# One more batch turned by DMA in a planned attention and mixture-of-experts kernel, with truer turn times in its planner and a new step order

## Chip, cores, metric

One core of one Trainium2 chip. The metric is the device time of one execution in microseconds (us). Where several runs are quoted, it is their median. All outputs are right.

The engines: PE is TensorE, PEld its weight loads, DVE VectorE, ACT ScalarE, POOL GpSimd, SPq the DMA queue of SyncE. A turn is a transposition by DMA, issued from SyncE. Small turns make xT (the attention output, turned) and rT (K and Q of the last 64 tokens), large ones make qkT (K and Q of half a batch).

## The reference, cut to what matters

```python
def phi(x):                                   # q, k, v: 8 batches, 8 heads, 576 tokens, 64 columns
    proj = x @ w_phi                          # 64 -> 128
    proj = proj - max(abs(proj), axis=-1)
    return concat([exp(proj), exp(-proj)])
num = q_p @ (k_p.T @ v);  den = q_p @ sum(k_p)
x = (num / den).transpose(0, 2, 1, 3).reshape(4608, 512)
P = exp(x @ w_gate)                           # 8 rounds of row and column normalisation follow
out = sum over 8 experts e of  P[:, e] * (relu(x @ w1[e]) @ w2[e])
```

Attention has to be finished before the routing is known. Expert 0's matmuls need no routing, though, so the kernel mixes them into the attention as filling for TensorE (PE).

## The kernel before

Each step of the algorithm (one letter of a string) appends operations to a plan. A list scheduler in the kernel then fixes at build time the order in which each engine gets its instructions. So the order is frozen on the chip: an engine stands at the next instruction of its list until that one can go.

```python
class Links:                                   # the planner's model of the DMA queues
    ...
            a, b = (x[0][2] for x in self.line)
            all_ = (0.61 if a.turn else 0.84) / (a.unit + b.unit)
    ...
    def dma(queue, nbytes, rate, fn, r=(), w=()):
        speed, unit = LINK.get(rate, (rate, 40))
        ...
        o = plan.op(queue, 0.8 if queue == "POOL" else 0.6, 0.0, fn, r, w, (), nbytes / speed)
        o.turn, o.unit = rate == 148, unit
    ...
    def pair_c(b, pr, xb):                     # turns a head pair's attention output into xT
        if b in (3, 4, 5, 6,):
            dma("SP", 1 << 17, 148, lambda: nc.sync.dma_start_transpose(
                out=xT[:, pr, b * SM:(b + 1) * SM].rearrange("p (a c) -> p a c", c=128),
                in_=xb()[:, 0:NJ].rearrange("p a b -> p (a b)")), [(xb, 0), (xb, 1)], [("xT", b, pr)])
            return
        pxt = new("P1")
        for j in range(NJ):                    # four transposes on PE
            pe(128, lambda j=j: nc.tensor.transpose(
                bf(pxt)[:, j * 128:j * 128 + 128], xb()[:, j, :], ident), ...)
        dve(270, lambda: nc.vector.tensor_copy(out=xT[:, pr, ...], in_=bf(pxt)[:, 0:512]), ...)
    ...
    def load_qk(b, hh, nh, t, r=()):           # K and Q of half a batch; from batch 2 on POOL's queue
        ...
            dma("POOL", nh << 17, 230, lambda x=x, src=src: nc.gpsimd.dma_start(
                out=t["qk"]()[:, x, o:o + nh], in_=...), r, [(t["qk"], x, i) for i in keys])
    def turn_qk(t, pr=None):                   # turns them into qkT on SyncE, one large DMA
        ...
            dma("SP", 1 << 19, 148, lambda: nc.sync.dma_start_transpose(
                out=t["T"]()..., in_=t["qk"]()...), ...)
    ...
    def gates():                               # a load is held until these have run
        seen = order[:at[0]]
        return [("max", x, seen.count(n) - 1) for x, n in ((0, "q"), (1, "a")) if n in seen]
    def stage_l(n):
        b, i = 1 + n // 2, n % 2
        if b > 1:
            halves[b, i] = new_half(b, i)
        load_qk(b, 4 * i, 4, halves[b, i], gates())
        load_v(b, 4 * i, 4, halves[b, i], gates())
    ...
    order = (
        "lraeaepqbwlqaqawwabwmqlltnrbppnwqbppmrmanbqaqmwwacmpnpbccpwbtcnmqnaqbclupunm"
        ...
```

The K and Q loads stand in POOL's list between POOL's own arithmetic (a negation `m`, a multiply `v`), which ACT and PE need. And their target `qk` is a ring buffer: a load may go out only when the turn that reads the buffer's earlier content has landed.

The softmax here doesn't subtract the row's maximum and nothing guards it: scores larger than these inputs give would overflow.

## Time and profile before

| | before |
|---|---|
| time | 1027.87 us, 3 runs from 1026.58 to 1027.88 |
| span of the profiled run | 1026.8 us |
| busy share PE / DVE / ACT / POOL | 98 / 80 / 69 / 45 % |
| turns by DMA, of attention outputs | 16 of 1.19 us on SyncE |

Busy shares average over two regimes: up to some 210 us attention feeds PE through DVE, ACT and POOL; after 262 us PE is full and nothing else counts. What a change in the first regime is worth can only be read there, from what PE waits for. The lines are in the prediction below.

### The profile page before, as it was taken

Reading aid. Unit: us, or ns where it says so; the run is one execution under the profiler, and the core shown is the slowest. Engines: PE = TensorE matmul, PEld = TensorE weight load, DVE = VectorE, ACT = ScalarE, POOL = GpSimd, SP = SyncE. Lnnn points to the kernel's source line nnn. Section 1 sums busy time; section 2 is a strip of 40 time slices with the busy share of each in tenths; the row PEclk is TensorE's granted clock in tenths of the full one; section 3 lists DMA queues with packets and bytes.
Section 4 is the critical chain, followed back from the end, with each engine's and each line's share of the span. In section 5 each row is a group of like instructions: output and inputs, shape, how many; then the busy total and the mean of one; then the engine's idle time right before and its main releaser. Section 6 shows DMA issues by size and latency. Waiting matters only on the chain.

```text
span 1026.8 us, 24281 instructions
## 1 busy us (share of the span) xinstructions
PE 1008.1 (98%) x9469; PEld 837.9 (82%) x9504; DVE 823.5 (80%) x1600; ACT 703.9 (69%) x1530; POOL 458.5 (45%) x480
## 2 busy tenths in 40 slices
PE   7899999999999999999999999999999999999998
PEld 4666666645888888888888888888888888888886
DVE  7999989987888887787777877787778877787775
ACT  7999999834888766666666666666665666666663
POOL 5768664400334444444444434544444433444342
PEclk9999999999999999999999999999999999999999
DMA  9999978170232611161115211341116111614333
GB/s 235 192 197 179 177 137 130 37 154 19 85 104 85 124 42 42 47 129 43 48 46 112 54 43 42 75 102 42 42 46 131 42 42 43 130 36 125 133 124 124
DMA packets 112501, 96.03 MB, mean 94 GB/s; under 512 B 54145, under 2 KB 87041, under 8 KB 112385
## 3 DMA queue, kind: packets, MB, share of 16 engines
q1 hardware_dynamic: 80576, 70.55, 26.5%
q0 software_dynamic: 31648, 23.86, 16.6%
q8 instruction: 74, 1.21, 0.5%
q14 instruction: 43, 0.34, 0.1%
q10 hardware_dynamic: 160, 0.07, 0.0%
HBM read 94.98 MB, written 14.16 MB: 106 GB/s over the span
## 4 chain that ended last, share of the span: by engine, by line
PE 93%; ACT 2%; DVE 1%; DMA 1%; SPq 1%; issue 1%; POOL 0%; DVEq 0%; ACTq 0%
PE ps L1273 74%; PE ps L573 17%; PE ps L856 2%; DMA acc<-in_q_dram 1%; ACT q L569 1%; ACT k L569 0%; SPq L495 0%; ACT wx L569 0%; SPq L551 0%; PE ps L885 0%; DMA xd<-S 0%; DVE ps L864 0%; DVE hT L1305 0%; DVE m L565 0%; POOL wx L761 0%
## 5 line engine op out<-in xcount | busy, mean ns | idle before, releaser
L1428 POOL TENSOR_TENSOR acc<-acc,V 128x512 f32<-128x512 f32 x248 | 314.8, 1280 | 484.5 <-ACT V L1425 426.7
L1301 ACT COPY U<-ps 128x512 f32<-128x512 f32 x378 | 217.0, 586 | 166.2 <-PE ps L1273 150.9
L1305 DVE CUSTOM_DVE_ANT_0 hT<-ps,U 128x512 bf16<-128x512 f32 x378 | 254.6, 687 | 87.7 <-PE ps L1273 59.9
L1425 ACT ACTIVATE V<-ps,P 128x256 f32<-128x256 f32 x496 | 208.1, 473 | 90.7 <-PE ps L1273 82.1
L1413 DVE SCALAR_TENSOR_TENSOR acc<-ps,P,acc 128x256 f32<-128x256 f32 x372 | 159.1, 478 | 69.5 <-PE ps L1273 69.2
L1273 PEld LDWEIGHTS <-S 128*128 128x128 bf16 x1984 | 194.1, 98 | 22.6 <-issue 0.2
L1273 PEld LDWEIGHTS <-T 128*128 128x128 bf16 x1512 | 148.0, 98 | 17.2
L1273 PEld LDWEIGHTS <-hT 128*128 128x128 bf16 x1488 | 145.6, 98 | 16.8
L1273 PE MATMUL ps<-X,T 128*128 128x256 bf16 x1008 | 152.4, 273 | 0.0
L1273 PE MATMUL ps<-T,S 128*128 128x256 bf16 x1056 | 135.8, 273 | 0.0
L1273 PEld LDWEIGHTS <-wx 128*128 128x128 bf16 x1152 | 112.7, 98 | 13.6 <-issue 0.2
L1181 DVE TENSOR_TENSOR S<-hT 128x1024 bf16<-128x1024 bf16 x124 | 87.2, 712 | 10.1 <-ACT hT L1310 9.9
L1273 PEld LDWEIGHTS <-w 128*128 128x128 bf16 x864 | 84.5, 98 | 9.8
L1273 PE MATMUL ps<-xT,wx 128*128 128x256 bf16 x576 | 88.4, 273 | 0.1
L1273 PE MATMUL ps<-X,wx 128*128 128x256 bf16 x576 | 86.8, 273 | 0.0
L1310 ACT ACTIVATE hT<-ps 128x512 bf16<-128x512 f32 x126 | 73.2, 606 | 9.8 <-PE ps L1273 9.8
L1273 PE MATMUL ps<-wx,hT 128*128 128x256 bf16 x560 | 77.6, 273 | 0.0
L1273 PE MATMUL ps<-xT,T 128*128 128x256 bf16 x504 | 76.7, 273 | 0.0
L573 PE MATMUL ps<-xT,w 128*128 128x512 bf16 x270 | 70.5, 379 | 0.7
L573 PE MATMUL ps<-w,hT 128*128 128x512 bf16 x276 | 69.8, 379 | 0.7 <-ACT q L569 0.2
L1273 PE MATMUL ps<-T,hT 128*128 128x256 bf16 x496 | 69.2, 273 | 0.0
L1273 PE MATMUL ps<-xT,w 128*128 128x256 bf16 x432 | 66.5, 273 | 0.0
(129 smaller groups left out, 1426.5 us busy)
## 6 DMA issues: line engine op xcount, KB each, us to landing
X<-xd SPq DMA_DIRECT2D x126, 256.0 KB, 2.7
wx<-in_moe_w_dram POOLq DMA_DIRECT2D x8, 1024.0 KB, 12.4
v_m<-in_v_dram SPq DMA_DIRECT2D x15, 512.0 KB, 5.6
out_dram<-acc SPq DMA_DIRECT2D x14, 512.0 KB, 2.9
w<-in_moe_w_dram POOLq DMA_DIRECT2D x6, 1024.0 KB, 12.1
xd<-S SPq DMA_DIRECT2D x18, 256.0 KB, 2.1
qk<-in_k_dram POOLq DMA_DIRECT2D x12, 256.0 KB, 5.5
qk<-in_q_dram POOLq DMA_DIRECT2D x12, 256.0 KB, 6.4
```

Source lines behind the costliest of these rows:

```text
L569: act(el, lambda: nc.scalar.activation(out=dst(), in_=src(), func=ACT.Exp, bias=0.0, scale=scale), r, w)
L573: nc.tensor.matmul(out_, lhsT=lhsT, rhs=rhs, start=start, stop=stop)
L856: pe(65, lambda j=j: nc.tensor.matmul(pn()[:, j * D1:j * D1 + D1], lhsT=s["T"][x]()[:, j % 2, 2 * h + j // 2, :] if j < 4 else r["T"][x]() ...
L1181: lambda: f.tensor_tensor(out=out_(), in0=x(), in1=y(), op=op), r, w, **kw)
L1273: pe(256, lambda i=i, k=k, z=z: nc.tensor.matmul(bank()[:, 256 * i:256 * i + 256], lhsT=lhs(k, i), rhs=rhs(k), start=first and z, stop=k = ...
L1301: act(512, lambda: nc.scalar.copy(out=u[fp][n]().rearrange("p a b -> p (a b)"), in_=x[fp]()), [x[fp]], [u[fp][n]])
L1305: dve(515, lambda: nc.vector._custom_dve(ADD_SAT, out=out_(fp, i, j), in0=bank[fp]().rearrange("p (a b) -> p a b", a=2), in1=u[fp][n](), s ...
L1310: act(512, lambda: nc.scalar.activation(out=out_(fp, i, j), in_=x[fp]().rearrange("p (a b) -> p a b", a=2), func=ACT.Relu, bias=0.0, scale ...
L1413: dve(320, lambda n=n, ts=ts: nc.vector.scalar_tensor_tensor(out=acc[g][:, ts, 256 * j:256 * j + 256], in0=bank()[:, 256 * n:256 * n + 256 ...
L1425: act(370, lambda n=n: nc.scalar.activation(out=u()[:, n, :], in_=bank()[:, 256 * n:256 * n + 256], func=ACT.Copy, bias=0.0, scale=P[:, 4 ...
L1428: pool(695, lambda: nc.gpsimd.tensor_tensor(out=acc[g][:, 2 * i:2 * i + 2, 256 * j:256 * j + 256], in0=acc[g][:, 2 * i:2 * i + 2, 256 * j: ...
```

## The change

The intent was to take 16 transposes from PE, to let the planner know how long a turn really holds SyncE, and to search a step order for that plan.

```diff
-            all_ = (0.61 if a.turn else 0.84) / (a.unit + b.unit)
+            all_ = (0.56 if a.turn else 0.84) / (a.unit + b.unit)
...
-        o = plan.op(queue, 0.8 if queue == "POOL" else 0.6, 0.0, fn, r, w, (), nbytes / speed)
+        dur = 0.8 if queue == "POOL" else 0.6 if rate != 148 else 2.4 if nbytes > 1 << 18 else 1.25
+        o = plan.op(queue, dur, 0.0, fn, r, w, (), nbytes / speed)
...
-        if b in (3, 4, 5, 6,):
+        if b in (2, 3, 4, 5, 6,):
...
-        load_qk(b, 4 * i, 4, halves[b, i], gates())
-        load_v(b, 4 * i, 4, halves[b, i], gates())
+        held = gates() if n else []
+        load_qk(b, 4 * i, 4, halves[b, i], held)
+        load_v(b, 4 * i, 4, halves[b, i], held)
...
     order = (
-        "lraeaepqbwlqaqawwabwmqlltnrbppnwqbppmrmanbqaqmwwacmpnpbccpwbtcnmqnaqbclupunm"
+        "arpqbwaaelwqwleaanmqwcbpwpqlnwbbrpeaqmqammnnqbbbcarctwcpplmtpmunlqnwcpnbtuau"
...   (four more lines of the string, all different)
```

More of the change, by code (lines that the diff above doesn't have):

```diff
@@ L1053 @@
     order = (
-        "lraeaepqbwlqaqawwabwmqlltnrbppnwqbppmrmanbqaqmwwacmpnpbccpwbtcnmqnaqbclupunm"
-        "taumquglcapalbcpnqqdcenmucugbblnapmrcqdutabnqpmunpbambccddnqplanmqmducpblttb"
-        "augnaqlnrbdcampcadmqeutunqcppmdcaqtdqabpbbmlrqtdnpmuaqualbnagnacctbmqulupran"
-        "tdpmtdqcmdnpdabdancpcabbqmpumqbcdgnappqunburqcbugmmnqdcdanumupqbnucmcpnmbddp"
-        "bqmpncncubncmmgccg"
+        "arpqbwaaelwqwleaanmqwcbpwpqlnwbbrpeaqmqammnnqbbbcarctwcpplmtpmunlqnwcpnbtuau"
+        "aqcpqunldamqblapnmcctadtuapqlalbmbgrgnuapalqaubmbmtcuqmpnbcdmnpdaqbccdrtqupq"
+        "nubnlnuqempgccupmanaclpadtbmadcqbdmpnqtdrbtqbdcnpuqbmlpmnuglndqpnbcamdapqnbu"
+        "cauamdcmrtuqmdndqpbumacbpunmgdpacqnuqpdtpbmndacbcbcagqcnpnurqumubpqmmbnbamcd"
+        "dcupmqcgncpbncnmcg"
     )
```

## The prediction

> **What bounds the kernel now.** I read the page's first two parts first, for who is busy and when.
>
> ```profile
> PE 1008.1 (98%) x9469; PEld 837.9 (82%) x9504; DVE 823.5 (80%) x1600; ACT 703.9 (69%) x1530; POOL 458.5 (45%) x480
> PE   7899999999999999999999999999999999999998
> DVE  7999989987888887787777877787778877787775
> ACT  7999999834888766666666666666665666666663
> POOL 5768664400334444444444434544444433444342
> PEclk9999999999999999999999999999999999999999
> ```
>
> TensorE is at work in 98% of the span at the full clock. Only its first two slices (51 us) are below 9 tenths. The second view is the table of stretches, where I cut the front finely:
>
> ```profile
> 0.00:10.00 10.00, 6.08 (x32) 4.45 (x33) 6.29 (x12) 5.28 (x11) 1.30 (x8) 1.00 0.74 205
> 10.00:20.00 10.00, 7.08 (x46) 4.17 (x44) 8.57 (x15) 8.89 (x26) 9.37 (x14) 1.00 1.20 285
> 20.00:30.00 10.00, 8.35 (x121) 6.08 (x120) 9.16 (x21) 9.47 (x25) 5.66 (x13) 1.00 1.25 246
> 30.00:40.00 10.00, 7.92 (x102) 6.32 (x99) 9.63 (x22) 9.74 (x25) 7.41 (x12) 1.00 1.23 134
> 40.00:50.00 10.00, 9.06 (x110) 5.96 (x109) 9.88 (x24) 10.00 (x27) 7.84 (x15) 1.00 1.35 189
> 50.00:60.00 10.00, 9.47 (x122) 6.90 (x124) 9.96 (x26) 10.00 (x25) 8.35 (x14) 1.00 1.08 209
> 60.00:70.00 10.00, 9.57 (x130) 6.67 (x129) 9.49 (x22) 8.94 (x22) 7.02 (x11) 1.00 1.07 171
> 262.00:1027.00 765.00, 760.22 (x6931) 677.93 (x6929) 591.75 (x1063) 486.75 (x1018) 324.63 (x260) 1.00 0.30 76
> ```
>
> Columns: stretch, length, then busy us and instructions of PE, PEld, DVE, ACT and POOL, then clock, DMA share and GB/s. From 20 to 70 us DVE and ACT have hardly a free moment (DVE 48.1 and ACT 48.2 of 50 us) while PE has holes: there PE waits for the attention chain and has no expert matmul to put between. From 262 us on PE is full, and that is three quarters of the span.
>
> Busy time includes the modelled tail of each matmul, so I also took the distance from one matmul's start to the next in the trace's records. The medians are 56 ns for 128 bf16 columns, 109 ns for 256 and 216 ns for 512. With 25 ns for the smallest, 109 ns for the fp32 transposes and columns/2.4 + 2.5 ns for the rest, the matmuls sum to 989.3 us. The first starts at 3.7 us. The last starts 4.9 us before the end. What is over, 1026.8 - 989.3 - 3.7 - 4.9 = 28.9 us, is holes between starts: 10.8 us before 30 us, 20.3 us before 70 us, 28.4 us before 260 us, and 0.4 us in all the rest. Between 70 and 260 us it is a steady 0.2 to 0.9 us in each 10 us.
>
> The third view is who PE waited for, cut at 70 us. Up to there:
>
> ```profile
> PE ps L703 <- DMA acc<-in_k_dram: 3.7, 1, 3.7
> PE ps L573 <- DVE wx L565: 1.9, 3, 1.4
> PE ps L703 <- ACT em_r L569: 1.1, 1, 1.1
> ```
>
> The first is the first input (the lead of 3.7 us), the others are DVE and ACT. For 70 to 262 us the same view is empty: no wait of PE there is long enough to be listed. So a DMA turn, a late V load or a late weight load costs PE nothing visible after 70 us.
>
> **What the Trainium skill says.** "TensorE: Matmul & The Clock Gate", section Back-to-back issue gap, gives N/2.4 + 2.5 ns for an isolated stream and 81 ns at N=128 for weight-load/matmul pairs. The trace agrees with the first (56, 109, 216 ns), and not with the 81 ns: the transposes here have a weight load each and still stand 56 ns apart. "VectorE: DVE Perf Modes", section The three transpose paths, puts a 128x128 bf16 transpose at 390 ns on TensorE and 1309 ns by DMA; the trace has 219 ns as the latency on TensorE, and a DMA turn of four such blocks occupies SyncE for 1.19 us and lands after 4.2 us. "DMA: Bandwidth & Descriptors", section DMA Transpose (X-bar), says that the plain transpose is issued from Sync or Scalar only and that two transposing streams must not be in flight together; here all are on SyncE, before and after, so there is one stream. The same page, section Issuing engines are not separate DMA queues, calls the issue time usually small against the transfer; here it is not:
>
> ```profile
> L879 SPq DMA_TRANSPOSE xT<-xb x10: 1190/1194/1403, 96.0 to 189.9; - x10
> L518 SPq DMA_TRANSPOSE qkT<-qk x12: 1322/1867/4506, 45.4 to 171.8; - x12
> L637 SPq DMA_TRANSPOSE rT<-qk_r x6: 1189/1506/3892, 27.1 to 131.9; - x6
> ```
>
> These are shortest, median and longest ns on SyncE. The kernel's planner booked 600 ns for each, so its planned order was wrong by 0.6 us for a small turn and by 1.3 us for a median large one.
>
> **The change part by part.** (1) Batch 2's attention output is turned by DMA as batches 3 to 6 are. Counting the built programs: 16 transposes and their 16 weight loads leave PE, four 128x512 copies leave DVE, four DMA turns are added on SyncE; nothing else changes in number on any engine.
>
> ```profile
> L885 PE MATMUL ps<-ident,xb x40: 216/219/222, 39.3 to 195.7; 128*128 128x128 bf16 x40
> L888 DVE COPY xT<-ps x16: 383/415/426, 41.9 to 204.2; 128x512 bf16<-128x512 bf16 x16
> ```
>
> PE: 16 x 56 ns = 0.9 us of stream, in a stretch where PE is full: this reaches the end. DVE: 4 x 0.415 = 1.7 us, at 80 to 95 us where DVE is 95% busy but PE does not wait for it: little of it reaches the end. SyncE: 4 x 1.19 = 4.8 us more, spread over a queue that has gaps of 1 to 4 us between its turns: off the path.
>
> (2) The planner's turn times (1.25 and 2.4 us, and a lower joint rate while a turn is in flight) add no instruction. They move SyncE's order: turns and V loads are sequenced as they really run. No PE wait after 70 us names a DMA, so the direct worth is near zero.
>
> (3) The hold. In the kernel before, the K/V load of batch 1 stands first in the step order, so its hold list is empty anyway. In the changed one it stands tenth; without the new rule it would wait for a maximum. With the rule SyncE's first 24 issues are the same in both programs. So this part allows the new order and gains nothing by itself.
>
> (4) The new step order is what can move the front. I laid the durations of the trace before over both instruction orders (sums, no replay). In front of the first expert up-projection stand 26.0 us of PE stream before, 25.3 after; of ACT records 57.7 and 56.5 us; and in front of the last batch 0 copy that it needs, 44.6 and 45.3 us of DVE records. In front of the eighth group: PE 38.6 and 37.9, ACT 75.0 and 71.9. In front of the twelfth: PE 50.3 and 52.9, ACT 90.3 and 93.5. Batch 1's last copy has 70.8 us of DVE records ahead before, 65.0 after. So the first group starts about when it did (46.3 us now), the middle comes some 2 to 3 us earlier on ACT, and the twelfth is even. The order reshuffles the front more than it shortens it. Also, the first weight load of expert 0 now goes out on POOL's queue ahead of the rest loads of batches 2 and 3, so the weights can't be the thing that is late; that queue's traffic at 10 to 20 us is not larger.
>
> Sum: 0.9 us of PE stream, plus 0 to 2 us fewer holes before 70 us (I choose 0.7, since the DVE count gets 0.7 longer while the ACT count gets up to 3 shorter), plus 0.2 us in the stretch from 70 to 205 us. 1027.9 - 1.8 = 1026.1 us.
>
> **The rivals.** (a) The front is shortened in earnest: if the holes before 70 us fall from 20.3 to about 17 us, as the ACT count at the eighth group allows at most, the sum is 0.9 + 3.3 = 4.2 us and the time 1023.7. For it: that order was searched with truer times. Against it: the DVE count in front of the first group, and that DVE and ACT are full there in any order. (b) A new wait takes the gain: a turn lands 4.2 us after issue and queues behind large turns that hold SyncE for up to 4.5 us, so xT of batch 2 comes some 4 to 8 us after its attention is done instead of about 1 us (0.22 + 0.42, with the waits). If PE then has nothing else, it shows as a wait on a DMA at 80 to 110 us; I allow 1 to 2 us, and the time would be 1027 to 1028. Against it: the list of PE's waits is empty there now, with 16 turns in the same queue. (c) The weight load that goes out earlier competes with the batch 1 loads, when the DMA share is already above 1 (two queues at once). Should the first transposes of the second half of batch 0 come 1 to 2 us later, everything shifts by that: 1027 to 1028. (d) Nothing moves after 205 us: routing on DVE and the first split products follow with PE full; a shift of 1 us either way leaves PE full.
>
> **Range and chances.** 0.9 us is sure. Around it lie the front (-3.3 to +2) and the queue (0 to +2). That gives 1023.3 to 1028.6 for 8 times in 10. 2% is 20.6 us, as large as all holes before 70 us together; PE's stream of 988.4 us can't shrink. So faster by 2% has a chance of 0.005, slower by 2% (a stall of 20 us) 0.01, within 2% 0.985.
>
> **What would show it right or wrong.** PE count down by 16, DVE by 4, 20 xT turns of 1.19 us on SyncE. The stretches 0 to 70 us: PE idle within 1.5 us of now (12.5 us), DVE and ACT still full. PE's waits after 70 us: still none of note; a wait on xT or rT from a DMA there would prove (b). First expert matmul at 45 to 48 us; if it comes before 44 us, (a); if after 49 us, (c). From 262 us on: the same 765 us. The prediction is wrong if the front's holes change by more than 3 us.

## The result, and the profile after

Before 1027.2 us (6 runs, 1026.36 to 1027.88), after 1028.82 us (6 runs, 1028.09 to 1031.25). A ratio here and below is the mean time of one kernel's fast runs over that of the other's fast runs of the same rounds, so it is not quite the ratio of the medians. It is 1.002, 95% interval 1.0007 to 1.0033. By the 2% measure that is "same", as predicted, but the sign is wrong and 1028.82 lies 0.2 us outside the range. The change costs about 2 us instead of saving 1.8.

Busy parts and slices of the changed kernel (this profiled run was the slowest of its six):

```profile
PE 1009.2 (98%) x9449; PEld 837.6 (81%) x9488; DVE 824.0 (80%) x1596; ACT 704.5 (68%) x1530; POOL 459.1 (45%) x480
PE   7899999999999999999999999999999999999998
ACT  7989999944877766666665666666666666666663
```

Nothing is to be seen at this scale: 2 us are a twentieth of one slice. But one thing is wrong in both kernels' first traces. The changed program has 9488 matmuls and PE shows 9449; before has 9504 and showed 9469. So 39 records are missing here and 35 there. Where I had summed the distances between matmul starts, each missing record had looked like a hole; the stream of 989.3 us in the prediction is short by the same amount, 7.6 us against 996.9 us in a complete trace. So I had both kernels traced again (before_again and after_again, the first two experiments), and both traces are complete. From here on "holes" are the starts' distances less 56, 109 or 216 ns per matmul (25 to 31 ns for the smallest), in complete traces, so they contain waits and matmuls that ran slower than that.

Stretches, before_again first, then after_again (start and end, length, then busy us and count of PE, PEld, DVE, ACT, POOL; clock, DMA share, GB/s):

```profile
40.00:50.00 10.00, 9.53 (x121) 6.51 (x120) 9.93 (x25) 10.00 (x29) 8.05 (x16) 1.00 1.36 188
70.00:80.00 10.00, 10.00 (x130) 6.99 (x128) 9.45 (x22) 10.00 (x27) 7.90 (x12) 1.00 1.04 213
262.00:1020.00 758.00, 758.00 (x6913) 675.71 (x6910) 589.75 (x1059) 484.76 (x1014) 324.17 (x260) 1.00 0.29 75
```

```profile
40.00:50.00 10.00, 8.45 (x96) 5.24 (x95) 9.52 (x21) 10.00 (x28) 8.96 (x15) 1.00 1.49 178
70.00:80.00 10.00, 9.31 (x90) 5.91 (x91) 8.28 (x16) 8.85 (x21) 8.56 (x15) 1.00 1.21 203
262.00:1020.00 758.00, 757.91 (x6923) 677.11 (x6921) 590.11 (x1062) 488.20 (x1019) 325.01 (x260) 1.00 0.29 75
```

The tail is full in both. The loss sits at 40 to 80 us: PE 8.45 of 10 us in place of 9.53, then 9.31 in place of 10. In the second stretch DVE and ACT fall too (9.45 to 8.28, 10.00 to 8.85), so something else held up all three. Who waited for the large K/Q turns says what, for this stretch. The lines are those of the turn's source line, before_again first (its list of waiters is empty), then after_again:

```profile
L518 SPq DMA_TRANSPOSE qkT<-qk x12: 1322/2608/5167, 42.4 to 169.8; - x12
who waited for it (us, times):
busy tenths in 40 slices 0000000000000000000000000000000000000000
DMA to landing us min/median/max: 4.3/6.9/9.7
```

```profile
L519 SPq DMA_TRANSPOSE qkT<-qk x12: 1694/3428/4132, 47.2 to 166.5; - x12
who waited for it (us, times):
  POOL qk L502: 2.5, 2
  PEld L574: 0.9, 1
  PE ps L574: 0.4, 1
DMA to landing us min/median/max: 4.7/6.3/8.4
```

The turns land as slowly in both (median 6.9 and 6.3 us). Before, nobody noticed. Now PE waits for one, and so does POOL, which wants to load into the buffer that the turn still reads. The chain of waits of after_again (start, length, what; parts left out):

```profile
62.80 7.46 DMA qkT<-qk
...
70.81 0.43 POOL qk L502
...
72.42 1.06 POOL vrd L684
...
78.57 0.68 PE ps L574 x16
```

A turn issued at 62.80 us lands at 70.2, only then may POOL's loads go out (70.81), and POOL's arithmetic behind them reaches PE at 78.57. The spare time from a turn's landing to its first use on PE does not tell the two kernels apart: it is 0.04 us in after_again for this turn and for the last xT of batch 2 (landed at 95.88 us), but in before_again it is 0.05 us for a turn that lands at 170.19 us, and at 36.6 us a weight load waits 0.36 us for an rT. What differs is that in after_again PE itself has nothing else to do at 70 us, and that POOL stands too.

### The profile page after: what moved, and what is told of

It reads as the page before. It is cut to its first block, busy times and chain, and to the rows that moved or that the text cites. A ratio compares the mean times of both kernels' runs of the same rounds, so it can differ in the third digit from the quotient of the medians.

```text
span 1029.4 us, 24231 instructions
## 1 busy us (share of the span) xinstructions
PE 1009.2 (98%) x9449; PEld 837.6 (81%) x9488; DVE 824.0 (80%) x1596; ACT 704.5 (68%) x1530; POOL 459.1 (45%) x480
## 4 chain that ended last, share of the span: by engine, by line
PE 91%; DMA 3%; DVE 2%; ACT 1%; POOL 1%; issue 1%; SPq 0%; POOLq 0%; DVEq 0%
PE ps L1275 74%; PE ps L574 15%; PE ps L857 1%; DMA qkT<-qk 1%; DMA xT<-xb 1%; POOL qk L502 1%; ACT q L570 0%; DMA acc<-in_q_dram 0%; DVE m L566 0%; ACT k L570 0%; PE ps L704 0%; DVE wx L566 0%; DVE ps L865 0%; DVE xb L871 0%; PE ps L886 0%
## 5 line engine op out<-in xcount | busy, mean ns | idle before, releaser
L1430 POOL TENSOR_TENSOR acc<-acc,V 128x512 f32<-128x512 f32 x248 | 315.4, 1282 | 483.2 <-ACT V L1427 426.7
L1415 DVE SCALAR_TENSOR_TENSOR acc<-ps,P,acc 128x256 f32<-128x256 f32 x372 | 159.1, 478 | 69.8 <-PE ps L1275 69.5
L1275 PEld LDWEIGHTS <-wx 128*128 128x128 bf16 x1152 | 112.7, 98 | 13.6 <-issue 0.2
L574 PE MATMUL ps<-w,hT 128*128 128x512 bf16 x275 | 69.5, 379 | 0.6
```

Source lines behind the costliest of these rows:

```text
L574: nc.tensor.matmul(out_, lhsT=lhsT, rhs=rhs, start=start, stop=stop)
L1275: pe(256, lambda i=i, k=k, z=z: nc.tensor.matmul(bank()[:, 256 * i:256 * i + 256], lhsT=lhs(k, i), rhs=rhs(k), start=first and z, stop=k = ...
L1415: dve(320, lambda n=n, ts=ts: nc.vector.scalar_tensor_tensor(out=acc[g][:, ts, 256 * j:256 * j + 256], in0=bank()[:, 256 * n:256 * n + 256 ...
L1430: pool(695, lambda: nc.gpsimd.tensor_tensor(out=acc[g][:, 2 * i:2 * i + 2, 256 * j:256 * j + 256], in0=acc[g][:, 2 * i:2 * i + 2, 256 * j: ...
```

## The experiments

Theory at the start: one part of the change is guilty by itself, first of all the fifth turned batch and its place in SyncE's list, which is rival (b) of the prediction. Its rivals: the truer costs alone, the new order alone, or (theory N) that a step order is good only for the very plan that it was found on, so that no part is guilty. The later theories, of single late inputs (theory L) and of a blocked queue, came from what the first runs showed. Where an expectation gives its theories letters, they stand for these: Q, O, G and C each blame one part or one place, N and L are as here; F says that an input which comes earlier is only waited for later.

### The whole change again, and before again

Edit: none.

> The changed kernel again, unchanged, to see its spread, since its profiled run was the slowest of its six. All theories: 1028.0 to 1029.5 us, ratio to the kernel before 1.001 to 1.002. If the profiled run is a typical one this time, the holes between matmul starts from 70 to 210 us should be about 9 us instead of the 11.2 us of the first trace, against 7.0 us before.

Measured: 1028.55 us (5 runs, 1028.21 to 1030.67), ratio 1.0019 [1.0006, 1.0032]. The small loss is real. The 9 us of holes expected at 70 to 210 us still counted missing records; this trace is complete and has 3.9.

> The kernel before, unchanged, for a second trace: the first one lacks 35 of the program's 9504 matmul records, and each missing record looks like a hole. If all are there, the matmuls sum to 996.9 us of stream and the holes to about 20 us, not 28.9, with hardly any from 80 to 200 us; against 23.1 us in the changed kernel's second trace. 1026.2 to 1027.7 us.

Measured: one look, 1026.52 us, with all 9504 records, as expected. The holes by stretch in complete traces (the first columns are us from the start; stream, holes and the 8 to 9 us before the first and after the last matmul make the span):

| kernel | 0-40 | 40-60 | 60-80 | 80-110 | 110-210 | later | holes | stream | span |
|---|---|---|---|---|---|---|---|---|---|
| before_again | 13.8 | 2.6 | 0.4 | 0.4 | 1.5 | 0.5 | 19.3 | 996.9 | 1024.7 |
| costs_only | 13.7 | 2.8 | 0.4 | 0.4 | 2.0 | 0.5 | 19.9 | 996.9 | 1025.5 |
| turn_only | 13.6 | 2.6 | 1.0 | 10.7 | 4.0 | 0.8 | 32.7 | 996.0 | 1037.5 |
| after_old_order | 13.4 | 2.6 | 0.6 | 7.6 | 2.7 | 0.8 | 27.7 | 996.0 | 1032.2 |
| order_only | 13.0 | 3.5 | 2.9 | 1.3 | 5.0 | 0.5 | 26.2 | 996.9 | 1031.7 |
| after_4_batches | 13.5 | 3.6 | 2.8 | 1.1 | 6.0 | 0.7 | 27.6 | 996.9 | 1033.0 |
| after_old_costs | 13.5 | 3.6 | 3.7 | 1.5 | 3.5 | 0.5 | 26.3 | 996.0 | 1030.5 |
| after_again | 13.4 | 3.6 | 2.2 | 0.8 | 2.1 | 0.9 | 23.1 | 996.0 | 1027.2 |

The stream falls by 0.9 us, as predicted, and the holes grow by 3.8 us. The rows between are the next experiments.

### The parts, alone and in mixtures

**turn_only.** Batch 2 turned by DMA, nothing else.

```diff
-        if b in (3, 4, 5, 6,):
+        if b in (2, 3, 4, 5, 6,):
```

> The kernel before with the one part 'batch 2 turned by DMA', old step order, old planner costs. Theory Q (the four more turns overload SyncE's turn path and make xT and qkT land late): slower than before by 1 to 2 us, 1028.2 to 1029.2, with PE waits on DMA xT or qkT after 70 us. Theory O (the new step order is at fault, the turns are harmless): 0.9 us of PE stream is saved, 1026.0 to 1027.2. Theory N (any new plan moves the time by 1 to 2 us in either direction, parts don't add up): anything from 1025 to 1030.

Measured: 1038.09 us (4 runs), ratio 1.0109 [1.0096, 1.0122]: 11.2 us lost, six times the loss of the whole change and far above what any theory expected. SyncE's list in its trace (start, us, engine, line, operation):

```profile
83.35 5.17 SPq L518 DMA_TRANSPOSE qkT<-qk  x1
88.61 2.77 SPq L879 DMA_TRANSPOSE xT<-xb  x1
91.56 2.50 SPq L637 DMA_TRANSPOSE rT<-qk_r  x2
94.17 1.21 SPq L879 DMA_TRANSPOSE xT<-xb  x1
```

Turn stands behind turn without a gap to speak of, and the last one lands 5.3 us after its issue. PE waits 4.9 us for it, and 3.4 us for POOL's v at 105 us. The planner had seen none of this: run again from the kernels' source, its own planned end is 1022.96 us for this kernel and 1022.93 us for before.

**costs_only.** The two planner lines of the change, nothing else.

```diff
+            all_ = (0.56 if a.turn else 0.84) / (a.unit + b.unit)
+        dur = 0.8 if queue == "POOL" else 0.6 if rate != 148 else 2.4 if nbytes > 1 << 18 else 1.25
```

> The kernel before with the planner's new turn costs alone (old step order, four batches turned). Theory N (a step order is only good for the plan that it was searched on): slower than before by 1 to 8 us, although the costs are truer. Theory C (truer costs make a better plan whatever the order): 1025 to 1027 us.

Measured: 1027.62 us (4 runs), ratio 1.0008 [0.9993, 1.0023]. Alone, the costs do nothing that can be told from zero; N (1 to 8 us slower) and C (1025 to 1027 us) both miss. Run again, the planner shows why: the two programs differ in one swap on SyncE, of a large turn and the V load next to it, and in nothing else.

**after_old_order.** Costs and turn, with before's order and hold.

```diff
-        "arpqbwaaelwqwleaanmqwcbpwpqlnwbbrpeaqmqammnnqbbbcarctwcpplmtpmunlqnwcpnbtuau"
+        "lraeaepqbwlqaqawwabwmqlltnrbppnwqbppmrmanbqaqmwwacmpnpbccpwbtcnmqnaqbclupunm"
...
```

> The changed kernel with the old step order: new costs, five batches turned. N: slower by 3 to 12 us; the wait of 5 us for xT of batch 2 that the turn alone showed should be there again, unless the new costs move the turns ahead of it. C: 1026 to 1028.5 us.

Measured: 1035.22 us (4 runs), ratio 1.0081 [1.0066, 1.0096]. Knowing the turn's time saves 2.9 us of turn_only's loss and leaves 8. By the planner the two programs differ in that same swap on SyncE and in two K loads, each of which stands behind a multiply and a cast of POOL here and stood ahead of them in turn_only. There POOL stood 3.54 and 8.32 us on these two loads, and PE waited 3.4 us for the multiply behind the second; that wait is gone. PE has one long wait here. First the wait, then two stretches (columns as above; note the clock, third from the end), then POOL's list at the same time:

```profile
PE ps L574 <- ACT hT L935: 5.3, 1, 5.3
```

```profile
107.00:111.00 4.00, 4.00 (x21) 1.64 (x21) 1.67 (x4) 2.69 (x9) 1.82 (x3) 0.65 1.35 222
111.00:115.00 4.00, 4.00 (x33) 2.36 (x32) 3.20 (x8) 3.87 (x11) 2.59 (x5) 1.00 0.92 97
```

```profile
98.30 0.25 POOL L768 CAST v<-em 128x16 bf16<-128x16 f32 x1
104.30 0.84 POOL L502 DMA_DIRECT2D qk<-in_k_dram  x1 [5.75 <-DMA qkT<-qk]
105.90 0.27 POOL L760 TENSOR_SCALAR m<-m 128x8 f32<-128x8 f32 x1
```

POOL finishes a cast at 98.55 us and stands for 5.75 us on a K load, until the turn that holds its buffer lands (issued at 94.34, landed 9.4 us later with two loads of K and Q and one of V in flight beside it). Behind the load stands a negation of 0.27 us that ACT waits for, and PE waits for ACT. In that run's chain of waits a turn of xT (at 92.04 us) stands right ahead of it. So 5.3 us of PE hang on an instruction that has nothing to do with the turn. And the hole costs more than its length: after it, PE's clock is granted at 0.65 for 4 us, and 512-column matmuls start 427 ns apart instead of 216, five in a row, with one of 378 and one of 374 ns at the edges: 5 x 0.21 + 2 x 0.16 = 1.4 us more. The Trainium skill, "TensorE: Matmul & The Clock Gate", Part 1, says that TensorE falls to half its clock after an idle window of about 3.4 us and gives 426.7 ns for 512 columns there. The 427 ns agree, and in turn_only the stretch after its 5.1 us hole is granted 0.55. But shorter holes were enough here: in all 19 traces the granted clock fell to half, for 3.4 or 6.8 us, after each of the nine holes of 2.2 us or more (four of them, in after_loads_behind, after_no_hold, both_moves and old_order_two_behind, had 2.2 to 2.4 us), after none of those of 1.3 to 1.9 us, and once without a hole above 1.0 us (after_no_hold, at 42 us). The changed kernel's holes are under 2 us and none of them shows it.

**order_only.** The new order and the hold, four batches turned, old costs.

```diff
-        "lraeaepqbwlqaqawwabwmqlltnrbppnwqbppmrmanbqaqmwwacmpnpbccpwbtcnmqnaqbclupunm"
+        "arpqbwaaelwqwleaanmqwcbpwpqlnwbbrpeaqmqammnnqbbbcarctwcpplmtpmunlqnwcpnbtuau"
...
+        held = gates() if n else []
```

> The kernel before with the new step order and its hold rule alone (old costs, four batches turned). N: slower by 3 to 9 us. Theory G (the new order is good in itself and the rest spoils it): 1025 to 1027 us.

Measured: 1034.78 us (4 runs), ratio 1.0085 [1.0068, 1.0101], as N expected.

**after_4_batches.** The change without its fifth batch.

```diff
-        if b in (2, 3, 4, 5, 6,):
+        if b in (3, 4, 5, 6,):
```

> The changed kernel with batch 2 back on TensorE (four batches turned), new order, new planner costs, new hold rule. Q: the loss goes, 1026 to 1027.3 us. O: the loss stays, and 0.9 us of PE stream comes on top, 1028.5 to 1030.

Measured: 1033.72 us (5 runs), ratio 1.0067 [1.0055, 1.0079]. Taking the suspect out makes the changed kernel 5.2 us slower, which neither Q nor O expected. That the turn is guilty by itself falls with it.

**after_old_costs.** The change without the two planner lines.

```diff
-        dur = 0.8 if queue == "POOL" else 0.6 if rate != 148 else 2.4 if nbytes > 1 << 18 else 1.25
+        dur = 0.8 if queue == "POOL" else 0.6
...
```

> The changed kernel with the planner's old turn costs (0.6 us per turn, joint rate 0.61), everything else new. Q: the planner sends turns out as if they cost nothing, so PE's waits on turns grow, 1029 to 1031. O: like the changed kernel within 0.5 us, 1028 to 1029.5. N: anything.

Measured: 1030.37 us (6 runs), ratio 1.0041 [1.0028, 1.0053], inside Q's range; PE's waits on turns after 68 us are 1.5 (xT) and 1.3 us (qkT) where after_again has 0.4 us (qkT).

**after_no_hold.** The change with its hold rule taken back.

```diff
-        held = gates() if n else []
+        held = gates()
```

> The changed kernel with its hold rule for the first K/V load of batch 1 taken back, all else as in the change, so that this load, tenth in the new step order, waits for a maximum of batch 0. The planner then makes another order from the front on. The prediction said that the hold rule only allows the new order and gains nothing by itself. Theory of the fitted order (a step order is good only for the very plan that it was found on): 1033 to 1037 us, as for the other three mixtures with the new order; the kernel's own plan ends 7.4 us later than the changed kernel's. Rival, that only the load's own lateness counts: batch 1 comes late, PE waits for its input before 45 us, holes before 40 us grow by 2 to 7 us and the rest stays as in the changed kernel, 1030 to 1035 us. Second rival, that the rule is idle: 1028 to 1029.5 us.

Measured: 1038.73 us (5 runs, 1036.94 to 1048.89), ratio 1.0113 [1.0097, 1.013]. That is 1.7 us above the range of the fitted order and further above its rivals'. The profiled run was the slowest. PE's longest wait in it, and POOL's for the turned buffer (total, times, longest):

```profile
PE ps L857 <- ACT hT L935: 7.8, 1, 7.8
```

```profile
POOL qk L502 <- DMA qkT<-qk: 12.8, 2, 9.1
```

The same pair as in after_old_order, at another place (163 us). By this trace it is the planned order that moved, not the load of batch 1.

What follows from the parts: with the old order the fifth turn costs 11.2 us (old costs) or 7.6 us (truer costs); with the new order it saves 4.4 or 5.2 us. The new order costs 7.8 us with four batches and saves 7.7 us with five (6.1 and 6.7 with truer costs). These are differences of medians, partly of different calls, whose before differs by 0.1 us. Theory N holds in this form: a kernel with one of the two, the order or the fifth turn, is slower than the one with neither and than the one with both, and the order's kernel loses again when its costs or its hold are taken back. The table of holes adds where: every kernel with the new order pays 5.8 to 7.3 us at 40 to 80 us where the old order pays 3.0 to 3.6, and every kernel with the old order and the fifth turn pays 7.6 to 10.7 us at 80 to 110 us where the new order pays 0.8 to 1.5. The new order buys off the stall that the fifth turn makes, with some 3 us of front. The planner, run again from each kernel's source, had half of this: its planned ends are 1022.3 us for the changed kernel, but 1023.6 (after_old_costs), 1026.6 (after_4_batches), 1027.4 (order_only) and 1029.7 us (after_no_hold). So that the new order loses without its turn or its hold stood in the plan; that the old order loses with the turn did not (1023.0 us for turn_only and after_old_order, 1022.9 for before).

### Moves in a frozen order

To test single waits without a new plan, each engine's list was frozen and a few operations were moved in it, after planning:

```diff
         done = self.schedule()
+        self.move(done, ("w", 0), ("w", 1))      # w_later
+        self.move(done, ("l", 3), ("l", 2))      # qk_earlier; both_moves has both lines
```

Here `move` puts the first-named loads just behind the others in the list.

**w_later.** The first weight load, which the new order sends out ahead of the batch loads, goes back behind them.

> The changed kernel with every engine's planned order kept and one DMA moved: expert 0's first weight load goes out on GpSimd's queue just ahead of the second one (20 us) instead of at 8.7 us. Theory L (the loss against the kernel before is input data that lands late because of what was put ahead of it): PE's waits for the acc loads at 10 to 15 us (0.7 and 1.5 us) go, DVE's hole of 1.6 us there too; 0.5 to 1.6 us faster than the changed kernel, 1027.0 to 1028.0. Theory F (DVE and ACT are full in the front anyway, so earlier input is only waited for later): within 0.3 us of the changed kernel, 1028.2 to 1028.9.

Measured: 1029.27 us (6 runs, 1028.22 to 1034.43), ratio 1.0034 [1.0013, 1.0055]. The profiled run's holes fell by 0.9 us to 22.2, the median did not. So the early weight load is not it: it does delay the first inputs (rival (c): PE waits 1.5 us on a Q load in the front of after_again), but the holes before 40 us are 13.4 us with it, 13.0 without it and 13.8 in before_again, so it costs at most 0.4 us there. The median lies above the ranges of both theories.

**qk_earlier.** K and Q of batch 2's second half, which the changed kernel loads at 56 us and turns at 62.8 us with 0.1 us to spare, are loaded at 41 us.

> The changed kernel, planned order kept, two DMAs moved: the K and Q loads of batch 2's second half go out directly behind those of its first half (41 us, ahead of a weight load and four rest loads) instead of at 56.2 us. L: their turn goes out at about 56 us instead of 62.8 and lands before 64 instead of 70.2 us; the holes from 60 to 80 us fall from 2.2 us to under 1 us; 1.0 to 2.0 us faster than the changed kernel, 1026.5 to 1027.5. F: the wait moves to the next engine, within 0.4 us, 1028.1 to 1028.9.

Measured: 1032.29 us (6 runs, 1030.49 to 1036.11), ratio 1.0061 [1.004, 1.0082]: a miss. Two turns that had landed after 4.9 and 7.5 us now took 8.8 and 13.1 us, with the moved loads and others in flight beside them. The holes at 60 to 80 us did fall, from 2.2 to 1.1 us, but those at 40 to 60 us rose from 3.6 to 5.8.

**both_moves.**

> Both moves together. L: the sum, 1.5 to 3.3 us faster than the changed kernel, 1025.2 to 1027.0: level with the kernel before (1026.9) or up to 1.5 us ahead of it, as the 0.9 us of PE stream then counts. F: 1028 to 1029.

Measured: 1032.39 us (6 runs, 1029.69 to 1040.22), ratio 1.0062 [1.0027, 1.0096]. No better; PE has a new hole of 2.2 us at 53 us, and half the clock for 3.4 us after it.

These two misses turned the question round: not how late an input is, but who stands in line behind it. The trace of after_old_order had the clearest case.

```diff
         done = self.schedule()
+        self.behind(done, ("l", 9), 3)       # old_order_loads_behind, on after_old_order
+        self.behind(done, ("l", 10), 4)      # old_order_two_behind has both lines
```

Here `behind` moves the K and Q loads of one half behind that many of POOL's following arithmetic instructions. The built programs differ from after_old_order's in POOL's list alone.

**old_order_loads_behind.**

> This is after_old_order (batch 2 turned by DMA, truer costs, the step order of before) with each engine's order frozen and one edit: the K and Q loads of the second half of batch 5 go out on POOL's queue three instructions later, behind a negation, a multiply and a copy that do not need them. In after_old_order's trace POOL stood 5.75 us on these loads, because their buffer was held by a large DMA turn that landed 9.2 us after its issue, and PE's only long wait (5.3 us at 101 us) leads back through ACT to the negation behind the loads. Theory of the queue: the fifth turn costs little by itself; it delays the turn in front of an in-order queue, and the instruction behind it is what PE lacks. It expects the hole at 101 us to go, holes of 21 to 22.5 us in place of 27.7, and 1028.0 to 1030.5 us (after_old_order had 1035.2), a ratio of 1.001 to 1.003. Theory of the slow turn: turns and loads together are simply too slow here, so PE meets the next late thing (xT turned behind the large turn, or the late K/Q of the next half) within a few us: a hole of 3 to 5 us at 102 to 112 us, and 1033 to 1035 us. Theory of the order as a whole (only a search over orders can repair it): no single move helps, 1034 to 1036 us.

Measured: 1037.7 us (4 runs), ratio 1.011 [1.0095, 1.0125], slower than after_old_order. POOL's list in its trace:

```profile
100.40 0.23 POOL L777 TENSOR_SCALAR m<-m 128x8 f32<-128x8 f32 x1 [1.07 <-DVE m L583]
105.15 0.84 POOL L519 DMA_DIRECT2D qk<-in_k_dram  x1 [1.32 <-DMA qkT<-qk]
116.27 0.84 POOL L519 DMA_DIRECT2D qk<-in_k_dram  x1 [5.95 <-DMA qkT<-qk]
```

The negation now runs at 100.40 instead of 105.90 us, the load goes out when it can anyway, and the hole at 101 us is gone. But the next large turn took 10.4 us to land, POOL stands 5.95 us on the next half's load, and PE has a new hole of 5.47 us at 117 us. The median, above the ranges of all three theories, fits the rival ("the loss moves on") better than the queue.

**old_order_two_behind.**

> old_order_loads_behind with the same edit made once more, one half later: the K and Q loads of the first half of batch 6 go out behind the value multiply, the negation and the next multiply of POOL's queue, all other orders frozen. In old_order_loads_behind's trace the hole at 101 us was gone, but POOL stood 5.95 us at 110 us on the next loads (their buffer was held by a large turn that took 10.3 us to land), and PE had a hole of 5.47 us at 117 us on what stood behind them. Theory of the queue: this hole goes too; after it no more loads stand blocked in the trace, so 1029 to 1032 us (1037.7 less the 5.5, less what of the run-to-run lateness hangs on it). Theory of the slow turn (turns and loads are too slow together, the loss moves on): a third hole of 3 to 6 us between 118 and 150 us, and 1034 to 1038 us.

Measured: 1031.11 us (6 runs, 1029.05 to 1034.91), ratio 1.0042 [1.0028, 1.0057]. With both loads moved, no POOL wait on a turned buffer is left and PE's longest wait after 60 us is this:

```profile
PE ps L592 <- DMA xT<-xb: 2.2, 1, 2.2
```

Two pairs of loads put back in one list gave back half of after_old_order's loss: 0.42% in place of 0.81%, or 4.1 us (1035.22 less 1031.11). That speaks for the queue, with a correction: its holes come one after another, and repairing one alone showed nothing. A rival is not excluded: the next two large turns also landed sooner in this run (after 8.3 and 5.4 us; in old_order_loads_behind after 10.4 and 8.0), so lighter traffic beside them may have done a part. The longest wait that is left, 2.2 us, is the fifth turn itself: DVE finishes xb at 93.2 us, the turn takes 3.8 us to reach PE, and PE had nothing else. After this hole, too, the clock is granted at half for 3.4 us. By an estimate from these figures that is 2.2 us and up to 1.7 us more, of the 4.4 us (1031.11 less 1026.75) that this kernel still loses to before. That is rival (b) as the prediction described it.

**after_loads_behind.** The same kind of edit in the changed kernel: `self.behind(done, ("l", 4), 5)`.

> The changed kernel with each engine's order frozen and one edit of the same kind: the K and Q loads of the first half of batch 3, on which POOL stood 1.44 us at 70 us (their buffer is held by the large turn issued at 62.8 us, landing after 7.4 us), go out behind the five POOL instructions that follow them. In the changed kernel's chain of waits this turn, these loads and then the POOL work behind them are one unbroken line from 62.8 to 78.5 us. Theory of the queue: holes between 60 and 80 us fall from 2.2 to about 1 us, and the time by 0.8 to 1.5 us, to 1027.1 to 1027.8 us, level with the kernel before. Theory of the slow turn: the turn itself has landed too late (PE's wait on qkT at 70.2 us stays) and the later loads make the next turn late: 1028 to 1031 us. Theory of a fitted order: any move costs, above 1030 us.

Measured: 1034.8 us (6 runs, 1030.81 to 1039.0), ratio 1.0076 [1.0051, 1.0101]. The run was aimed wrong: I had miscounted the loads and moved those of batch 3's first half, out at 57.7 us, while POOL stands at 70 us on those of the second half. Moved to 62.8 us they share the queues with the turn issued at 63.8 us: PE's wait on qkT grows from 0.4 to 2.0 us, POOL's from 2.5 to 5.8 us. It says nothing of the intended repair (its time fits the third theory, that any move costs).

**after_loads_behind_2.** The right pair: `self.behind(done, ("l", 5), 5)`.

> after_loads_behind again, aimed right. That run moved the K and Q loads of batch 3's first half; the loads on which POOL stood 1.44 us at 70 us are those of its second half, two loads further on, and these are moved here behind the five POOL instructions that follow them, all orders frozen. Theory of the queue: POOL's wait of 1.44 us at 70 us goes, holes between 60 and 80 us fall from 2.2 to 1 to 1.5 us, 1027.2 to 1028.2 us. Theory of the slow turn: PE's waits at 70 us are on the turned K/Q itself, which these loads don't touch, and the moved loads make the next turn later: no gain, 1028.5 to 1031 us. Theory of a fitted order, in which any move costs: above 1031 us.

Measured: 1029.97 us (6 runs, 1028.9 to 1034.49), ratio 1.004 [1.0024, 1.0056], in the range of the slow turn. POOL's wait of 1.44 us at 70 us is gone; holes at 60 to 80 us are 2.8 us where 2.2 were. PE's only wait there is now another:

```profile
PE ps L591 <- POOL v L785: 1.7, 1, 1.7
```

The negation was no longer held up by the loads, but now it waits for DVE, and the displaced loads (0.8 us of POOL each, three in a row) stand in front of the multiply that PE needs. In the changed kernel each engine is planned up to the next one's need, so a repair opens the next wait.

**after_loads_behind_w.** This and w_later's move together.

> after_loads_behind_2 with w_later's edit beside it (the first weight load of expert 0 moved back to just ahead of the second one, so that the front's loads have the queues to themselves). If both late inputs cost, as the traces say (0.4 to 0.9 us each), the two together give 1026.5 to 1027.7 us, which would be level with or below the kernel before. If a repair at one place only moves the lateness on, 1028.5 to 1031 us.

Measured: 1030.46 us (6 runs, 1028.4 to 1032.62), ratio 1.0037 [1.0025, 1.0049]. The same. No version that I ran beats before.

## Why the prediction was wrong, point by point

- **Part (1), 0.9 us of PE stream.** Right: 996.0 against 996.9 us in complete traces, 16 transposes fewer. What the 1.7 us of DVE copies are worth no run shows apart. The 20 turns of batch outputs are there, at a median of 1.19 to 1.20 us on SyncE (one took 2.16). That they are "off the path" failed: in after_again PE waits for a turn at 70 us, and POOL stands 1.44 us on the buffer of the same turn.
- **Part (2), truer costs worth near zero.** Right alone (+0.7 us, interval across zero). With the fifth turn they save 2.9 us under the old order and 1.8 us under the new one. "No PE wait after 70 us names a DMA" was a fact of before, not of the kernel with the turn.
- **Part (3), the hold gains nothing by itself.** Right in its wording: with the old order the rule leaves the program as it was. With the new order it belongs to the plan (after_no_hold is 12 us slower than before).
- **Part (4), the front: 0.7 us fewer holes before 70 us.** The failed step. In complete traces the holes before 70 us are 16.7 us before and 18.2 us after: 1.5 us more (0.6 us of them are the hole that begins at 69.5 us, ahead of the late turn). PE's idle time there grows by 2.4 us (busy 60.5 and 58.1 of 70 us), beyond the 1.5 us that the prediction allowed. Counting how much DVE and ACT work stands ahead of a group said when a group can start, not whether the next input is there. The first expert matmul came at 45.1 us, inside the range named.
- **0.2 us fewer holes at 70 to 205 us.** The second failed step: from 70 to 210 us they are 2.0 us before and 3.9 us after, 1.8 us more before rounding. With 1.5 and 1.8 us in place of -0.7 and -0.2, the sum is -0.9 + 1.5 + 1.8 = +2.4 us, against +2.5 us of span between the two complete traces.
- **The 28.9 us of holes.** Wrong by the missing records: 19.3 us in the complete trace. The "steady 0.2 to 0.9 us in each 10 us" at 70 to 260 us was mostly them. From 70 to 210 us PE had 2.0 us to gain at most. The 20.3 us "before 70 us" are what that trace has before 80 us; before 70 us it has 19.8. Two smaller slips: the last slice of PE's line reads 8, as the second does, and the range's lower end, 1023.3, lies below the sum of the best terms, 1023.7.
- **Rival (b)** came true in kind, not in place or size. PE and POOL wait for a turn, but for K and Q at 70 us, where the rival named xT at 80 to 110 us. A wait on xT there shows only in the first, slower trace (0.6 us at 97 us); the holes at 80 to 110 us grew by 0.4 us, and 1028.8 lies above its 1027 to 1028. As described it happened under the old order (PE waits 4.9 us on xT in turn_only). I gave it too little weight because PE's list of waits was empty. An empty list says that nothing is late; it does not say by how little: before_again's is empty from 70 to 262 us, and at 170 us a turn lands 0.05 us ahead of its use.
- **Rival (c)** shows in its waits (1.5 and 0.7 us on the first inputs), not in the front's sum. **(a)** did not happen. **(d)** is right: 758.0 and 757.9 us of PE in the 758 us from 262 us on.

Shown by runs: the interaction of order and turn, and that under the old order half of its loss goes when two pairs of loads stand further back in POOL's list. Only argued from traces: that the changed kernel's own loss is the same tightness spread over several engines; two repairs aimed at single waits there gave nothing back. Open: the 1.0 us at 40 to 60 us that all four kernels of the table with the new order share, which no run repaired (the waits of PE that after_again lists there are on ACT and DVE, 0.2 to 0.5 us each), and what makes a turn land after 2.3 us or after 10.4 us. Counted over all 19 traces, a turn of xT that was issued with no transfer but turns in flight landed after 2.5 us (median of 87), with one after 4.0 us (126), with two after 4.8 us (82), with three or more after 6.8 us (65). But no run took the loads away.

## What to carry to other kernels

In a kernel whose engine lists are frozen, count the slack of every transfer (landing to first use) and look at what stands behind each DMA issue in its engine's list; an empty list of waits hides both. (A small slack alone cost nothing: before_again had 0.05 us at one turn.) A step order fits one plan: a part and the order that was searched for it, each taken alone, can cost several times what both together do, so judge them together. Where the planner runs off the chip, compare its lists and planned ends first: here they showed that the costs alone swap two issues, and which mixtures lose by plan. Before summing holes from a trace, compare its record count with the program's.

## What the Trainium skill lacked or had wrong

- "DMA: Bandwidth & Descriptors", Issuing engines are not separate DMA queues: issue time "is usually small relative to the DMA itself". Here a small turn holds SyncE for 1.19 us of a landing of 2.3 us at best, and a large one (after_old_order, 94 us) held it for 5.7 us of 9.4 us.
- The same page, DMA Transpose (X-bar), has nothing on how long a turn takes beside other loads: in the 19 traces small ones landed after 2.3 to 12.0 us, large ones after 4.2 to 14.2 us.
- "VectorE: DVE Perf Modes", The three transpose paths: 390 ns for a 128x128 block on TensorE; the trace has 219 ns of latency and 56 ns between starts, which decides what a block taken from TensorE saves.
- "TensorE: Matmul & The Clock Gate", Back-to-back issue gap: 81 ns for weight load and matmul pairs at 128 columns; here 56 ns. Its Part 1 is borne out in the 427 ns at 512 columns, and not in the idle window of about 3.4 us: half the clock came after holes of 2.2 to 2.4 us in four traces, and not after holes of 1.3 to 1.9 us.
- No page that I read warns that matmul records can be missing from a trace: 35 of 9504 looked like 7.6 us of idle TensorE (996.9 us of stream in the complete trace, 989.3 us without them).
- "Perfetto Trace Analysis", Identifying Dependency Chains, tells to read an instruction's waits; no page that I read warns of unrelated work behind a waiting DMA issue in the same engine's list. Here POOL stood up to 9.1 us on such an issue (after_no_hold).
